# Linear attention and gated convolution FFN in one kernel: w_in loaded in three column blocks, identity between the first loads, an ordered factor product, another instruction order

## The chip, the cores and the metric

The kernel runs on one core of a Trainium2 chip. The core has TensorE (PE, with its weight loads shown as PEld), VectorE (DVE), ScalarE (ACT), GpSimd (POOL), SyncE (SP) and 16 DMA engines. The metric is the device time of one execution in microseconds; lower is better. "Time" is the whole execution; "span" is from the first to the last instruction of the profiled one.

## The reference

Eight batches, eight heads, 576 positions, head dimension 64; a model width of 512 and a hidden width of 1024. All inputs and the output are float32.

```python
kv  = einsum('bhsd,bhse->bhde', k, v)            # 64 x 64 per batch and head
out = einsum('bhsd,bhde->bhse', q, kv)
rms = sqrt(mean(out * out, axis=-1) + 1e-6)
x   = (out / rms * g_norm)                       # heads side by side: (b, 576, 512)

h    = maximum(x @ w_in, 0)                      # (b, 576, 1024)
conv = sum_k conv_w[k] * shift(h, k - 1)         # 3 taps along the positions, zero padded
y    = (h * sigmoid(conv)) @ w_out               # (b, 576, 512)
```

## The kernel before

**Layout.** A position s is split as s = p * 6 + r, so that q, k and v are loaded with 96 partitions (p) and six runs r of 64 values per head. POOL's queue loads them and casts float32 to bfloat16 on the way (`load`, L146 to L152). PE contracts k and v over the positions (`kv`, L263), two heads at a time into a 128 x 128 block diagonal `kvbd` (`kvc`), transposes q by an identity matrix (`qt`, L287; copied out by `qc`), and multiplies (`ot`, L310). The product has the model width on the partitions (four tiles t of 128) and the positions in the order (r, p) along the free dimension. `natural` (L315) is the view that reads them in the order p * 6 + r.

**Norm.** For batches 1 to 7 the squares (`sq`) are summed by PE (`ss`), ACT takes Ln and Exp (`ln`, `ex`), DVE splits the factors into bfloat16 parts (`sl`), PE spreads them over the partitions (`sp`), and DVE multiplies (`mu`, L415) into `xT`. Batch 0 has a shorter path, tile by tile: `sq`, a matmul with a block of ones (`on`), `nl` (Ln) and `nx` (Exp) over the full tile, and the product `mu0` (L358), which reads the product in PSUM and the factor `rs0` in SBUF, both in the order (r, p), and writes `xT` in the natural order, that is in steps of six bfloat16 values.

**FFN.** g_norm is folded into w_in: `ws` (L257) scales a staged float32 tile of w_in into the bfloat16 `w_in_sb`. `hm` (L427) is one 128-wide slice f of x @ w_in, `re` the relu. The convolution is done by PE for batch 0 (`di` builds diagonal matrices, `cv`, `sv`, `mv`: matmul, sigmoid, product) and by DVE for the others (`ta` three taps, `ad` two sums, `sg` sigmoid on ACT, `mg` product), in groups of one or two batches (CONV, L59). `om` multiplies a tile of 128 rows with w_out, `ea` evacuates it on ACT, `st` stores it from SP.

**Order.** Every engine runs its instructions in the order in which the program lists them. The program is a prologue (loads, constants) and then the list `ORDER` (L62 to L106), a text of some 640 tokens, each of which calls one of the functions above: `hm.3.5` is `hm(3, 5)`. The loop at L541 walks through the list, and the code at L546 ties each engine's instructions to that order. So the list sets the order on each of the engines and queues. PSUM is shared by two pools: `ps_a` with three buffers (qt, ot, on, sp, hm, cv) and `ps_b` with two (kv, ss, om, cw_ps).

**The prologue, before.** POOL issues q of batch 0 and then k and v in four chunks each (nine DMAs), makes the identity `ident` and a small float32 `ident32` (each a memset and an affine select, shown as masks.py lines), and then issues w_in as eight tiles of 128 x 512 float32 into the buffers `row` (L160). SP loads g_norm and the convolution weights (`cw_rows`). PE's first instruction transposes `cw_rows` by `ident32` into `cw_ps` (L207); DVE copies it to `cw` and derives `spread`, `ng`, `na`, `nb` from `ident` (L208 to L227). Activation tables are loaded by ACT when the function set changes (`act_table`, L229; "ln" and "sig").

Of the kernel before, what the change touches and what calls it, by code (L numbers as in the profile page):

```python
# [72 lines left out]
cv.0.3 sv.0.3 mv.0.6 sq.2.0 hm.1.1 re.1.1 ot.2.2 mv.0.7 ot.2.3 oc.2.3 mv.0.3 om.0.0 oc.2.2 ta.1.2 ta.1.3
ea.0.0 sq.2.2 Lv.3 Lq.3 ad.1.3 sg.1.3 kv.3.0.4 kvc.3.0.4.1 qt.3.1 Lk.4 ad.1.1 qc.3.1 qt.3.0 Lv.4 kvc.3.0.4.0
ot.3.3 qc.3.0 sg.1.1 mg.1.1 sq.2.3 sq.3.3 ot.3.2 oc.3.2 ot.3.1 oc.3.3 ta.1.4 sq.3.2 ta.1.5 om.0.2 sq.3.1
ad.1.2 ot.3.0 sq.3.0 hm.1.0 re.1.0 ss.2 ss.3 ln.1 ex.1 mg.1.3 ea.0.2 kv.4.0.4 Lq.4 Lk.5 Lv.5 sl.1 sp.2.0
mu.2.0 oc.3.1 oc.3.0 sp.3.0 sp.2.3 mu.3.0 om.0.3 mu.2.3 sp.2.2 mu.2.2 kvc.4.0.4.1 sp.2.1 mu.2.1 qt.4.1 sg.1.2
qc.4.1 ea.0.3 sp.3.1 om.0.1 kvc.4.0.4.0 ot.4.3 oc.4.3 sq.4.3 mu.3.1 sp.3.3 mu.3.3 hm.2.0 re.2.0 sp.3.2 qt.4.0
mu.3.2 qc.4.0 ot.4.2 hm.2.3 ta.1.0 ea.0.1 oc.4.2 sq.4.2 Lq.5 re.2.3 ot.4.0 oc.4.0 hm.2.1 ot.4.1 sq.4.0
kv.5.0.4 oc.4.1 re.2.1 ta.1.1 ad.1.0 hm.3.0 sq.4.1 kvc.5.0.4.0 Lk.6 re.3.0 kvc.5.0.4.1 sg.1.0 qt.5.0 st.0.0  # L80
qc.5.0 hm.2.2 re.2.2 mg.1.0 ot.5.0 oc.5.0 sq.5.0 qt.5.1 Lv.6 hm.3.3 Lq.6 Lk.7 Lv.7 re.3.3 qc.5.1 ot.5.2 oc.5.2
sq.5.2 hm.3.1 re.3.1 hm.3.7 Lq.7 re.3.7 ot.5.3 sq.5.3 mg.1.2 hm.3.4 re.3.4 ta.2.0 ta.2.1 ad.2.0 hm.3.2 oc.5.3
re.3.2 ot.5.1 sq.5.1 kv.6.0.4 ta.2.2 oc.5.1 ss.4 ss.5 ln.2 ex.2 ta.2.3 hm.3.5 re.3.5 hm.2.5 re.2.5 hm.2.4
re.2.4 sl.2 kvc.6.0.4.0 qt.6.1 qc.6.1 sp.4.0 qt.6.0 sp.5.1 mu.4.0 kvc.6.0.4.1 sg.2.0 om.0.7 qc.6.0 ot.6.1
mu.5.1 sp.4.3 mu.4.3 sp.5.2 ea.0.7 om.0.8 mu.5.2 oc.6.1 ot.6.0 hm.3.6 st.0.3 sq.6.1 ad.2.1 sq.6.0 sp.4.2
mu.4.2 ea.0.8 kv.7.0.4 sp.4.1 mu.4.1 oc.6.0 re.3.6 st.0.7 mg.2.0 ot.6.2 sg.2.1 kvc.7.0.4.0 sq.6.2 hm.2.6
re.2.6 qt.7.0 qc.7.0 st.0.2 kvc.7.0.4.1 oc.6.2 om.0.4 ea.0.4 ot.7.1 ot.6.3 ot.7.0 om.0.5 sq.6.3 ta.2.4 ta.2.5
# [22 lines left out]
def kernel(  # L110
# [43 lines left out]
    w_stage = {}  # L154

    def load_w_in(half):
        for t in range(NT):
# [2 lines left out]
            nc.gpsimd.dma_start(out=st, in_=moe_w_in[t * P:(t + 1) * P, half * 512:(half + 1) * 512])  # L160
# [424 lines left out]
```

## Time and profile before

| | |
|---|---|
| median of three runs | 217.47 us (217.29 to 218.61) |
| the profiled execution | 216.95 us, of which 215.2 us are the span |
| granted TensorE clock, mean | 0.992 |
| PE, DVE, ACT busy | 178.4, 158.3, 153.4 us |
| activation table loads | 10 (one in the prologue at L181, nine at L232) |
| HBM read, written | 32.52 MB, 9.44 MB |

A page of the profile gives busy times per engine, the span in 40 slices of 5.4 us with the busy share in tenths, the chain of work that ended last, and the groups of instructions by line. In a group's row stand line, engine, operation, output and input, shape and count, then the busy time in us and the mean of one in ns, then the idle time just before them and what ended it. "Idle before" is inferred from semaphores: a wait for several things is put down to the one that came last.

### The profile page before, as it was taken

How to read it: one execution, taken by the hardware profiler on the slowest of the kernel's cores; microseconds unless marked ns; L12 is line 12 of the kernel's file. 1: busy time of each engine (PE TensorE's matmuls, PEld its weight loads, DVE VectorE, ACT ScalarE, POOL GpSimd, SP SyncE). 2: the span in 40 equal slices, each digit the busy share in tenths (PEclk: the TensorE clock that was granted, in tenths of full speed). 3: DMA queues.
4: the chain of work that ended last, by engine and by line, in shares of the span. 5: the costliest groups of instructions: out<-in, count | busy, mean ns of one | idle time of the engine just before them, and what ended most of it. 6: DMA issues, size and time to landing. Idle time of an engine off the chain costs nothing.

```text
span 215.2 us, 4372 instructions
## 1 busy us (share of the span) xinstructions
PE 178.4 (83%) x1783; PEld 111.5 (52%) x1801; DVE 158.3 (74%) x328; ACT 153.4 (71%) x232; POOL 28.9 (13%) x47
## 2 busy tenths in 40 slices
PE   0246469957997839999989999999999999999993
...
DMA  5999999997089999399702000214130000324773
GB/s 61 198 322 263 204 206 204 138 201 116 3 121 202 213 182 186 82 138 196 111 5 97 3 0 0 101 41 155 49 149 0 0 3 0 148 97 154 282 269 126
DMA packets 25992, 27.03 MB, mean 126 GB/s; under 512 B 1372, under 2 KB 20852, under 8 KB 25972
## 3 DMA queue, kind: packets, MB, share of 16 engines
...
q1 hardware_dynamic: 5380, 9.45, 11.6%
q8 instruction: 14, 0.23, 0.5%
...
HBM read 32.52 MB, written 9.44 MB: 195 GB/s over the span
## 4 chain that ended last, share of the span: by engine, by line
DVE 39%; PE 37%; ACT 15%; issue 4%; DMA 3%; POOL 0%; POOLq 0%; ACTq 0%; DVEq 0%
PE h_ps L433 14%; PE om_ps L523 12%; DVE tap L458 12%; DVE tap L466 6%; DVE tap L465 5%; DVE h L478 4%; PE qt_ps L294 3%; DVE xT L360 3%; DMA q_sb<-in_q_dram 3%; PE cv_ps L499 3%; ACT sq L326 3%; ACT h L439 3%; DVE xT L416 3%; PE sp_ps L410 2%; ACT L232 2%
## 5 line engine op out<-in xcount | busy, mean ns | idle before, releaser
L433 PE MATMUL h_ps<-xT,w_in_sb 128*128 128x288 bf16 x512 | 70.1, 291 | 4.1 <-DVE xT L360 1.3
L523 PE MATMUL om_ps<-w_out_sb,h 128*128 128x512 bf16 x280 | 65.2, 385 | 0.8 <-issue 0.2
L433 PEld LDWEIGHTS <-w_in_sb 128*128 128x128 bf16 x512 | 50.0, 99 | 20.4 <-issue 5.4
L439 ACT ACTIVATE h<-h_ps 128x576 bf16<-128x576 f32 x64 | 40.2, 652 | 14.2 <-PE h_ps L433 13.7
L458 DVE TENSOR_SCALAR tap<-h,cw 128x576 bf16<-128x576 bf16 (+1 forms) x120 | 43.1, 425 | 4.2 <-ACT h L439 3.7
L523 PEld LDWEIGHTS <-h 128*128 128x128 bf16 x288 | 28.4, 99 | 33.4 <-issue 2.4
L472 ACT ACTIVATE tap<-tap 128x1152 bf16<-128x1152 bf16 (+1 forms) x20 | 30.9, 1547 | 3.9 <-DVE tap L466 3.7
L529 ACT ACTIVATE row<-om_ps 128x512 f32<-128x512 f32 x36 | 21.4, 594 | 17.1 <-PE om_ps L523 16.3
L416 DVE TENSOR_TENSOR xT<-o,sp_ps 128x576 bf16<-128x576 f32 x28 | 20.0, 748 | 6.0 <-PE sp_ps L410 6.0
L478 DVE TENSOR_TENSOR h<-h,tap 128x1152 bf16<-128x1152 bf16 (+1 forms) x20 | 19.8, 992 | 2.1 <-ACT tap L472 2.1
L466 DVE TENSOR_TENSOR tap<-tap 128x1150 bf16<-128x1150 bf16 (+1 forms) x20 | 20.1, 1004 | 0.7
L332 ACT ACTIVATE o<-o_ps 128x576 f32<-128x576 f32 x28 | 17.8, 659 | 3.3 <-PE o_ps L307 2.6
L465 DVE TENSOR_TENSOR tap<-tap 128x1150 bf16<-128x1150 bf16 (+1 forms) x20 | 19.8, 991 | 0.0
L326 ACT ACTIVATE sq<-o_ps 128x576 bf16<-128x576 f32 x28 | 17.7, 660 | 0.5 <-PE o_ps L307 0.5
L301 DVE COPY qT<-qt_ps 128x1152 bf16<-128x1152 bf16 x16 | 11.8, 751 | 6.9 <-PE qt_ps L294 6.9
L150 POOL DMA_DIRECT2D k_sb<-in_k_dram x11 | 8.0, 730 | 53.7 <-PE kv_ps L270 53.7
L284 ACT ACTIVATE kvbd<-kv_ps 64x256 bf16<-64x256 f32 (+1 forms) x18 | 6.1, 341 | 12.3 <-PE kv_ps L270 11.2
L306 PE MATMUL o_ps<-qT,kvbd 128*128 128x64 bf16 x32 | 6.3, 196 | 7.8 <-DVE kvbd L282 3.1
L410 PE MATMUL sp_ps<-wparts,spread 128*128 128x288 bf16 x56 | 10.0, 287 | 2.9 <-DVE wparts L401 2.7
L294 PE MATMUL qt_ps<-ident,q_sb 96*64 96x96 bf16 x384 | 11.5, 217 | 0.3
L232 ACT ACT_TABLE_LOAD x9 | 11.5, 1283 | 0.1
L294 PEld LDWEIGHTS <-q_sb 96*64 96x64 bf16 x384 | 9.8, 117 | 2.2 <-issue 2.1
...
## 6 DMA issues: line engine op xcount, KB each, us to landing
...
```

Of the source, the lines that this page charges most:

```text
L294: nc.tensor.transpose(ps[i * D:(i + 1) * D, tt, r * PS:(r + 1) * PS], q_sb[:, 2 * (2 * u + tt) + i, r * D:(r + 1) * D], ident[:PS, :PS])
L326: nc.scalar.activation(s.rearrange("p (n r) -> p n r", r=R), natural(src), AX.Square)
L416: nc.vector.tensor_mul(x_tile(b)[:, t, :].rearrange("p (e n) -> p e n", e=2), T["o32", b, t].rearrange("p (e n) -> p e n", e=2), T["sp", b ...
L433: nc.tensor.matmul(ps[:, e, :HS], w_in_sb[:, t, f * P:(f + 1) * P], x[:, t, e * HS:(e + 1) * HS], start=(t == 0), stop=(t == NT - 1))
L439: nc.scalar.activation(h_tile(b // 2)[:, f, b % 2, :].rearrange("p (e n) -> p e n", e=2), T["hm", b, f][:, :, :HS], AX.Relu)
L458: nc.vector.tensor_scalar_mul(tap[:, m, f % 2, :, :].rearrange("p b s -> p (b s)"), h_tile(p)[:, f, bs, :].rearrange("p b s -> p (b s)"), ...
L465: nc.vector.tensor_add(tap[:, 1, :, 1:], tap[:, 1, :, 1:], tap[:, 0, :, :S - 1])
L466: nc.vector.tensor_add(tap[:, 1, :, :S - 1], tap[:, 1, :, :S - 1], tap[:, 2, :, 1:])
L472: nc.scalar.activation(tap, tap, AX.Sigmoid)
L478: nc.vector.tensor_mul(h, h, T["tap", c, j][:, 1])
L523: nc.tensor.matmul(ps, h[:, f, m * P:(m + 1) * P], w_out_sb[:, f, :], start=(f == 0), stop=(f == NF - 1))
L529: nc.scalar.activation(T["os", p, m], T["om", p, m], AX.Copy)
```

## The change

- w_in is loaded as three column blocks (columns 0 to 255, 256 to 511, 512 to 1023), each one DMA for all 512 rows, into one staging tile of the pool tag `h`. The first is issued on SP's queue ahead of everything else there, the other two on POOL's queue behind k and v. `ws` scales a block at a time: three instructions instead of eight.
- DVE clears `ident` at the start; POOL's affine select follows the issue of q and stands ahead of k and v. `ident32` is a DVE copy of a corner of `ident`.
- `mu0` writes `xT` in order and reads its two inputs through `natural`.
- `ORDER` is replaced. The same functions are called with the same arguments, apart from `ws`. The list switches the activation table seven times instead of nine.

```diff
-di.5 qt.0.0 qc.0.0 qt.0.1 qc.0.1 kv.0.0.1 kvc.0.0.1.0 di.0 kv.0.1.1 kvc.0.1.1.0 kvc.0.0.1.1 ot.0.0 sq.0.0 di.6
-kvc.0.1.1.1 ot.0.1 sq.0.1 on.0 nl.0 nx.0 kv.0.2.1 kvc.0.2.1.1 kvc.0.2.1.0 on.1 kv.0.3.1 nl.1 nx.1 mu0.0 ot.0.2
-kvc.0.3.1.1 mu0.1 di.3 Lk.1 ws.3.0 Lv.1 kvc.0.3.1.0 ot.0.3 sq.0.2 ws.0.0 sq.0.3 on.2 nl.2 ws.1.0 nx.2 mu0.2
-ws.2.0 on.3 nl.3 nx.3 mu0.3 hm.0.0 re.0.0 di.7 Lq.1 ws.1.1 hm.0.2 ws.0.1 re.0.2 cv.0.0 sv.0.0 hm.0.1 re.0.1
-ws.2.1 ws.3.1 hm.0.5 re.0.5 di.2 cv.0.2 sv.0.2 hm.0.3 re.0.3 di.1 cv.0.1 mv.0.0 Lw sv.0.1 mv.0.2 cv.0.5 sv.0.5
-hm.0.7 kv.1.0.4 kvc.1.0.4.1 kvc.1.0.4.0 qt.1.1 qc.1.1 qt.1.0 qc.1.0 ot.1.3 re.0.7 oc.1.3 sq.1.3 Lk.2 Lv.2 Lq.2
-hm.0.4 re.0.4 ot.1.2 sq.1.2 ot.1.0 sq.1.0 mv.0.5 ot.1.1 sq.1.1 di.4 oc.1.2 mv.0.1 ss.1 ln.0 ex.0 sl.0 hm.0.6
-re.0.6 cv.0.7 oc.1.0 oc.1.1 sv.0.7 sp.1.0 mu.1.0 sp.1.2 mu.1.2 cv.0.6 sp.1.3 sp.1.1 mu.1.3 sv.0.6 Lk.3 cv.0.4
...
-re.5.1 mg.2.1 hm.5.0 re.5.0 st.0.4 hm.5.4 re.5.4 hm.4.4 re.4.4 ln.3 ex.3 ta.3.2 hm.4.6 mg.2.3 re.5.6 om.1.5
-ea.1.5 st.1.5 re.4.6 ta.3.3 om.1.6 ad.3.1 ea.1.6 sg.3.1 sl.3 ta.3.0 sp.7.0 sp.6.0 mu.7.0 sp.7.2 mu.7.2 om.1.7
...
+di.4 di.7 di.6 qt.0.0 qc.0.0 qt.0.1 kv.0.0.1 kvc.0.0.1.0 kvc.0.0.1.1 ot.0.0 di.5 kv.0.1.1 sq.0.0 qc.0.1 on.0
+di.2 kvc.0.1.1.0 nl.0 kvc.0.1.1.1 ot.0.1 sq.0.1 kv.0.2.1 nx.0 on.1 kvc.0.2.1.1 mu0.0 kvc.0.2.1.0 di.1 Lk.1
+Lv.1 nl.1 nx.1 kv.0.3.1 ot.0.2 kvc.0.3.1.1 sq.0.2 on.2 kvc.0.3.1.0 nl.2 mu0.1 ot.0.3 sq.0.3 on.3 ws.1 Lq.1
+ws.2 nx.2 mu0.2 nl.3 ws.0 nx.3 mu0.3 hm.0.0 hm.0.7 re.0.7 re.0.0 kv.1.0.4 kvc.1.0.4.0 Lw hm.0.5 Lk.2 Lv.2 Lq.2
+re.0.5 hm.0.2 re.0.2 qt.1.0 kvc.1.0.4.1 hm.0.4 re.0.4 qc.1.0 ot.1.0 qt.1.1 qc.1.1 ot.1.1 sq.1.0 oc.1.1 sq.1.1
+ot.1.2 sq.1.2 di.0 ot.1.3 sq.1.3 oc.1.3 oc.1.2 ss.1 ln.0 hm.0.1 Lk.3 ex.0 re.0.1 Lv.3 hm.0.6 di.3 Lq.3 oc.1.0
+hm.0.3 cv.0.0 re.0.6 sl.0 sp.1.0 mu.1.0 re.0.3 sv.0.0 cv.0.4 sp.1.1 kv.2.0.4 sv.0.4 Lk.4 sp.1.3 mu.1.1
+kvc.2.0.4.1 mv.0.0 mu.1.3 sp.1.2 mu.1.2 cv.0.6 cv.0.2 sv.0.6 hm.1.0 mv.0.6 qt.2.1 sv.0.2 mv.0.4 mv.0.2 qc.2.1
...
+oc.6.2 sq.6.2 ea.1.2 st.0.6 om.1.6 ot.7.0 sq.7.1 hm.4.4 om.1.8 sg.3.0 re.4.4 ea.1.6 sq.7.0 sq.7.3 ot.7.2
+st.1.2 ad.3.1 sq.7.2 ea.1.8 oc.7.3 om.1.3 ea.1.3 ss.6 ss.7 ln.3 hm.5.6 st.0.1 mg.3.0 ta.3.4 re.5.6 ta.3.5
+ad.3.2 om.1.4 hm.4.7 st.0.5 ex.3 om.1.0 oc.7.2 sl.3 oc.7.0 st.1.5 sp.6.0 mu.6.0 sp.6.3 re.4.7 mu.6.3 sg.3.1
...
-    from concourse.masks import make_identity
...
-    w_stage = {}
-
-    def load_w_in(half):
-        for t in range(NT):
-            st = work.tile([P, 512], FP32, name="row", bufs=BUFS["row"])
-            w_stage[t, half] = st
-            nc.gpsimd.dma_start(out=st, in_=moe_w_in[t * P:(t + 1) * P, half * 512:(half + 1) * 512])
-
+
+    W_COLS = ((0, 256), (256, 512), (512, 1024))
+    w_stage = work.tile([P, NT, D_ff], FP32, name="w_stage", tag="h", bufs=BUFS["h"])
+
+    def load_w_in(eng, i):
+        lo, hi = W_COLS[i]
+        eng.dma_start(
+            out=w_stage[:, :, lo:hi], in_=moe_w_in[:, lo:hi].rearrange("(t p) f -> p t f", p=P))
+
+    load_w_in(nc.sync, 0)
+    ident = consts.tile([P, P], BF16, name="ident")
+    nc.vector.memset(ident, 0.0)
     load("q", 0)
+    nc.gpsimd.affine_select(
+        out=ident, in_=ident, compare_op=AL.not_equal, fill=1.0,
+        base=0, pattern=[[-1, P]], channel_multiplier=1)
     for t in range(NT):
         load("k", 0, 2 * t, 2)
         load("v", 0, 2 * t, 2)
+    load_w_in(nc.gpsimd, 1)
+    load_w_in(nc.gpsimd, 2)
...
-    ident = consts.tile([P, P], BF16, name="ident")
-    make_identity(nc, ident)
     ident32 = consts.tile([3 * NF, 3 * NF], FP32, name="ident32")
-    make_identity(nc, ident32)
-    load_w_in(0)
-    load_w_in(1)
+    nc.vector.tensor_copy(ident32, ident[:3 * NF, :3 * NF])
...
     @op
-    def ws(t, half):
-        nc.vector.tensor_scalar_mul(
-            w_in_sb[:, t, half * 512:(half + 1) * 512], w_stage[t, half], g_sb[:, 0:1])
+    def ws(i):
+        lo, hi = W_COLS[i]
+        nc.vector.tensor_scalar_mul(w_in_sb[:, :, lo:hi], w_stage[:, :, lo:hi], g_sb[:, 0:1])
...
     @op
     def mu0(t):
-        x = x_tile(0)[:, t, :].rearrange("p (n r) -> p r n", r=R)
         nc.vector.tensor_mul(
-            x, T["ot", 0, t][:, :S].rearrange("p (r n) -> p r n", n=PS),
-            T["rs0", t].rearrange("p (r n) -> p r n", n=PS))
+            x_tile(0)[:, t, :].rearrange("p (n r) -> p n r", r=R),
+            natural(T["ot", 0, t][:, :S]), natural(T["rs0", t]))
```

More of the change, by code (lines that the diff above doesn't have):

```diff
@@ L73 @@
[L73 to L87, printed above, removed]
@@ new lines @@
+kvc.2.0.4.0 hm.1.1 re.1.0 re.1.1 ot.2.3 ta.1.0 cv.0.7 sq.2.3 sv.0.7 hm.1.4 Lv.4 oc.2.3 cv.0.5 qt.2.0 ta.1.1
+ad.1.0 re.1.4 sv.0.5 sg.1.0 hm.1.5 re.1.5 qc.2.0 ot.2.1 mg.1.0 cv.0.1 sq.2.1 sv.0.1 oc.2.1 ot.2.0 sq.2.0
+oc.2.0 kv.3.0.4 kvc.3.0.4.0 ta.1.4 Lq.4 qt.3.0 qc.3.0 hm.1.6 hm.1.7 kvc.3.0.4.1 ta.1.5 mv.0.7 re.1.6 re.1.7
+ot.3.0 oc.3.0 sq.3.0 mv.0.1 qt.3.1 cv.0.3 qc.3.1 ot.3.3 sv.0.3 oc.3.3 ta.1.6 Lk.5 Lv.5 ta.1.7 ot.3.2 sq.3.3
+sq.3.2 ot.3.1 oc.3.2 mv.0.3 ot.2.2 kv.4.0.4 sq.3.1 sq.2.2 oc.3.1 hm.1.2 ss.2 re.1.2 ss.3 ad.1.3 ln.1 ex.1
@@ new lines @@
+hm.3.5 re.3.5 ot.5.3 oc.5.3 sq.5.3 hm.3.2 hm.3.3 re.3.2 ot.5.0 hm.2.3 ta.2.4 re.3.3 sq.5.0 ta.2.5 re.2.3
+ot.5.2 sq.5.2 oc.5.0 oc.5.2 om.0.4 ot.4.0 ta.2.2 ot.5.1 hm.3.6 oc.4.0 ad.2.2 ta.2.3 sq.5.1 ea.0.4 sq.4.0
+om.0.5 ss.4 ss.5 oc.5.1 re.3.6 qt.6.0 ea.0.5 ln.2 qt.7.0 qt.6.1 ex.2 ad.2.1 qc.6.0 om.0.8 ea.0.8 sg.2.1 qc.6.1
+om.0.1 sl.2 sp.4.0 ea.0.1 sp.4.2 qc.7.0 sp.5.1 kv.6.0.4 mu.4.0 hm.3.0 mu.5.1 mu.4.2 mg.2.1 sp.5.0 hm.3.1
+mu.5.0 re.3.0 re.3.1 sp.4.3 kv.7.0.4 kvc.7.0.4.0 kvc.6.0.4.0 sp.5.3 kvc.7.0.4.1 hm.2.1 re.2.1 mu.4.3 ta.2.0
@@ new lines @@
+hm.2.6 sp.4.1 st.0.8 mu.5.3 kvc.6.0.4.1 sg.2.2 sp.5.2 ta.2.1 mu.4.1 om.0.7 hm.3.7 re.2.6 ad.2.0 mg.2.2 re.3.7
+sg.2.0 mu.5.2 om.0.6 hm.2.7 re.2.7 hm.4.0 ea.0.6 hm.5.1 ta.2.6 re.5.1 hm.4.3 re.4.3 ta.2.7 ea.0.7 hm.5.0
+re.5.0 re.4.0 hm.5.5 re.5.5 hm.5.2 re.5.2 st.0.3 ad.2.3 mg.2.0 st.0.7 qt.7.1 hm.4.1 hm.5.4 sg.2.3 re.4.1
+qc.7.1 re.5.4 hm.4.5 re.4.5 hm.4.2 ot.6.1 re.4.2 ta.3.0 oc.6.1 hm.5.3 sq.6.1 mg.2.3 ot.6.3 om.1.5 ot.6.0
+re.5.3 ot.7.1 oc.6.3 sq.6.3 ea.1.5 ot.6.2 sq.6.0 oc.7.1 om.1.2 ta.3.1 ta.3.2 oc.6.0 ta.3.3 ad.3.0 ot.7.3
```

34 lines of the change are left out of this document (16 added, 18 removed).

## The prediction

> **What bounds the kernel now.** I read the page first, then the busy times by stage, then the chain of waits of the first 30 us, then the groups by line.
>
> ```profile
> PE 178.4 (83%) x1783; PEld 111.5 (52%) x1801; DVE 158.3 (74%) x328; ACT 153.4 (71%) x232; POOL 28.9 (13%) x47
> PE   0246469957997839999989999999999999999993
> DMA  5999999997089999399702000214130000324773
> ```
>
> PE works 178.4 of 215.2 us, and nearly all its idle time lies in the first 15 of the 40 slices (80 us). The busy times by stage (us from the start; PE is the first busy column, then PEld, DVE, ACT, POOL, the granted clock, the DMA share and GB/s) put numbers on this:
>
> ```profile
> 0.00:9.50 9.50, 0.23 (x3) 0.19 (x3) 1.64 (x31) 1.28 (x1) 7.13 (x18) 1.00 0.85 120
> 9.50:29.30 19.80, 10.09 (x118) 5.40 (x119) 16.03 (x38) 8.74 (x16) 10.26 (x15) 1.00 1.22 252
> 29.30:52.00 22.70, 18.20 (x209) 12.73 (x210) 9.42 (x28) 17.91 (x28) 2.30 (x3) 1.00 1.19 183
> 52.00:80.00 28.00, 21.87 (x371) 15.62 (x373) 18.49 (x41) 23.01 (x40) 6.08 (x8) 1.00 0.87 136
> 80.00:145.00 65.00, 62.68 (x720) 41.29 (x728) 56.28 (x88) 58.29 (x91) 3.15 (x5) 0.97 0.45 79
> 145.00:201.00 56.00, 55.00 (x326) 31.90 (x327) 55.13 (x107) 38.91 (x51) 0.00 (x0) 1.00 0.22 83
> 201.00:215.20 14.20, 10.31 (x47) 4.40 (x45) 1.32 (x2) 5.22 (x8) 0.00 (x0) 1.00 0.59 224
> ```
>
> PE idles 9.3, 9.7, 4.5, 6.1, 2.3, 1.0 and 3.9 us in these seven stages. After 145 us PE and DVE are both full, so there a new order has nothing to win. What can be won lies before 80 us. The chain of waits of the first 30 us (start, length, what) says what holds the start:
>
> ```profile
> 1.29 6.11 DMA q_sb<-in_q_dram
> ...
> 8.60 0.29 POOL ident masks.py:199
> ...
> 9.60 0.18 DVE cw L208
> ...
> 12.07 0.57 DVE dg L487 x3
> ...
> 18.29 2.09 DVE xT L360
> ...
> 27.32 1.98 DVE xT L360
> ...
> 29.34 0.88 PE h_ps L433 x3
> ```
>
> q has landed at 7.40, but the identity, behind nine load issues on POOL, is ready only at 8.89. Then DVE prepares constants until 12.07 and scales conv diagonals (L487) before it serves q. From 18.29 the four products of batch 0 (L360) are the longest pieces, and the first matmul group of the FFN can finish only when the last of them ends, at 29.3.
>
> **The change part by part.** The groups by line (busy us, mean ns of one):
>
> ```profile
> L360 DVE TENSOR_TENSOR xT<-o_ps,o 128x576 bf16<-128x576 f32 x4 | 8.3, 2074 | 1.7 <-ACT o L350 1.7
> L416 DVE TENSOR_TENSOR xT<-o,sp_ps 128x576 bf16<-128x576 f32 x28 | 20.0, 748 | 6.0 <-PE sp_ps L410 6.0
> L332 ACT ACTIVATE o<-o_ps 128x576 f32<-128x576 f32 x28 | 17.8, 659 | 3.3 <-PE o_ps L307 2.6 <-PE qt_ps L294 0.6
> L324 ACT ACTIVATE sq<-o_ps 128x576 bf16<-128x576 f32 x4 | 2.6, 646 | 3.3 <-remote 2.9 <-PE o_ps L307 0.4
> L258 DVE TENSOR_SCALAR w_in_sb<-row,g_sb 128x512 bf16<-128x512 f32 x8 | 3.5, 483 | 0.0
> L346 ACT ACTIVATE o<-on_ps,eps_sb 128x576 f32<-128x576 f32 x4 | 3.0, 740 | 1.2 <-PE on_ps L307 1.2
> L350 ACT ACTIVATE o<-o 128x576 f32<-128x576 f32 x4 | 2.7, 683 | 0.1
> L232 ACT ACT_TABLE_LOAD x9 | 11.5, 1283 | 0.1
> L499 PE MATMUL cv_ps<-h,dg 128*128 128x288 bf16 (+1 forms) x48 | 7.5, 296 | 2.6 <-ACT h L439 1.7 <-DVE xT L416 0.7 <-ACT gate L507 0.2
> ```
>
> *The factor product (mu0).* It writes its 576 results in steps of 12 bytes and takes 2.07 us; L416 makes the same product of as many elements, written in order, in 0.75 us. The changed mu0 writes in order but reads both inputs in steps of 384 bytes. ACT reads PSUM in such steps (L332) in 0.66 us and in order (L324) in 0.65 us, so the step costs it nothing; DVE never reads so in this trace. Bounds: 0.75 us, and 2.07 us if the step costs on the read side what it costs on the write side, or somewhat more. I take 0.75, the same engine and operation. [...]
>
> *Identity and the SyncE block.* The rows for this part are the DMA rate in three single microseconds, and when w_in's rows and q were issued (length min/median/max in ns, first and last start) and landed:
>
> ```profile
> 2.00:3.00 1.00, 0.00 (x0) 0.00 (x0) 0.75 (x14) 0.03 (x1) 1.00 (x3) 1.00 0.13 6
> 11.00:12.00 1.00, 1.00 (x38) 1.00 (x36) 0.93 (x7) 0.01 (x1) 1.00 (x2) 1.00 1.30 197
> 13.00:14.00 1.00, 0.00 (x0) 0.00 (x0) 1.00 (x4) 0.00 (x0) 0.88 (x3) 1.00 1.01 410
> ...
> L160 POOL DMA_DIRECT2D row<-in_moe_w_in_dram x8: 537/538/1189, 9.2 to 13.8; - x8
> DMA to landing us min/median/max: 4.6/5.0/5.8
> ...
> L150 POOL DMA_DIRECT2D q_sb<-in_q_dram x3: 777/794/886, 1.3 to 20.5; - x3
> DMA to landing us min/median/max: 6.1/12.4/21.5
> ```
>
> The identity now follows q's issue (1.3 plus at most 0.9 us), so it is ready near 2.6 us by the 0.29 us of the old one; it pushes the k and v issues back 0.3 us, which hides in their queue. The block of w_in (512 KB) on SyncE's queue goes ahead of everything. The casting loads of q, k, v write 197 GB/s, the plain rows of w_in 410. 512 KB cost 1.3 us at 410 and 2.6 at 197; the engines are nearly idle before 3 us, so some of it is free: between 0 and 2.6, I take 1.0. q then lands at 8.4 and PE can start at once. g and cw_rows queue behind the block on SP and land, I estimate, near 6 us instead of before 9; PE's first instruction (cw_ps) waits for them, and behind it stand all of qt.0. If they land by 8 this is free. DVE's ident32 copy, new, waits for POOL's identity with the memsets of the constants behind it (1.64 us in the first stage); they end near 5 us and nobody needs them sooner. DVE's block behind cw (9.60 to 12.07, 2.5 us) then ends by 9, in the shadow of q. PE's first pieces, from two qt (48 matmuls) and two kv (24) to the first product with kvbd and the early matmuls of the FFN:
>
> ```profile
> 9.49 2.13 PE L294 MATMUL qt_ps<-ident,q_sb 96*64 96x96 bf16 x48
> 11.42 0.84 PE L270 MATMUL kv_ps<-v_sb,k_sb 96*64 96x64 bf16 x24
> ...
> 14.70 0.23 PE L306 MATMUL o_ps<-qT,kvbd 128*128 128x64 bf16 x1 [2.43 <-DVE kvbd L282]
> ...
> 25.76 1.12 PE L433 MATMUL h_ps<-xT,w_in_sb 128*128 128x288 bf16 x4 [0.83 <-ACT o L346]
> ...
> 27.38 0.66 PE L433 MATMUL h_ps<-xT,w_in_sb 128*128 128x288 bf16 x2 [0.50 <-DVE w_in_sb L258]
> ```
>
> That product started at 14.70. Now it starts two qt (2.1), one kv (0.4) and some 0.7 us for the copies and hand-offs behind q: 8.4 + 3.2 = 11.6 us. ACT then needs four times L324, L346 and L350 (2.07 us together): 8.3 us from 12.2, done near 21 with small gaps.
>
> *w_in in three pieces.* Its last bytes landed between 18.4 and 19.6 (13.8 plus 4.6 to 5.8); the bytes ahead of them in all queues are the same, so I take 19.0. Fewer issues on POOL (two instead of eight) gain nothing where DMA is full until 41 us. All of the scaling (3.5 us, taken as unchanged by the larger shapes) now stands before mu0.3: ws.1 and ws.2 (three quarters, 2.6 us) behind mu0.1, ws.0 (0.9) between mu0.2 and mu0.3. Before, half of it stood ahead. So DVE binds: 19.1 + 2.6 + 0.75 + 0.9 + 0.75 = 24.1 us for the last product, against 29.3. That is 5.2 us; but before, six of the eight matmuls of hm.0.0 had already run in the waits (25.76 and 27.38), worth 0.75 us of PE; now ws.0 comes too late for most of that. Net 4.5 us.
>
> *The order, 29 to 52 us.* ln.0 now stands ahead of sv.0.0, so the Ln table is still loaded, and two of the nine table loads fall away (2 x 1.28 us) in the stage where ACT works 17.9 of 22.7 us. These two pieces of the chain lie there:
>
> ```profile
> 45.84 1.28 ACT L232
> ...
> 50.49 0.77 DVE xT L416
> ```
>
> The load at 45.84 lies on the chain, and PE idled 4.5 us in this stage. Behind ss.1 now stand three hm (0.1, 0.6, 0.3), some 3 us that cover ln, ex and the split; three convolutions by matmul move behind sl.0 (3 x 6 x 0.296, at most 5.3 us) into the next stage. I take 2.0 of the 4.5 us.
>
> *52 to 80 us.* The moved convolutions fall where PE idles 6.1 us and ACT 5.0, so they cost nothing there unless that idle time goes to something else; I take a gain of 0.5. *After 80 us*: the same work in another order, all three engines nearly full: 0, from +1 to -3. At the end five om still stand behind the last mg, as before.
>
> *Loads.* They stay in the same order on POOL. The third q landed at 20.5 + 21.5 = 42.0; qt.2.1 will now want it near 43. So batch 2's load becomes the next thing that is late if the middle goes better than I think.
>
> The sum: 4.5 + 2.0 + 0.5 = 7.0 us off the profiled execution's 216.95 gives 209.95. The median of the runs shown is 0.5 above that execution, so I forecast 210.5.
>
> **The rivals.** A, the forecast (0.48): 210.5, by the bounds above 208.5 to 213.
>
> B, the later idle time closes too (0.18): the norm chain of batches 2 and 3 is covered as batch 1's is, and PE wins 4 of its 6.1 us between 52 and 80: 206.5. For it: there also PE waits while ACT works 23.0 of 28. Against it: ACT gets the deferred gates in that stage.
>
> C, mu0 stays at 2.07 us (0.14). DVE then runs mu0.1 18.4 to 20.5, ws until 23.1, mu0.2 to 25.2, ws.0 to 26.1, mu0.3 to 28.2: 4.1 us later than in A, 214.6. [...] With a read that costs still more, about 216.
>
> D, the start is won and lost again (0.12): after 80 us DVE idled 8.7 + 0.9 us and PE 2.3 + 1.0; any waits that the new order adds there count in full, and seven of them give 217.5. This is also the case that the change does not do what it says.
>
> E, slower (0.08): DVE starves ahead of sl.3. In the new order ta.3.0, ta.3.1, ta.3.4, ta.3.5, two ad and mg.3.0 stand ahead of sl.3 on DVE, and no longer behind it. If they wait on sigmoid or relu of a PE that is itself behind, sl.3 and so all of batches 6 and 7 (mu, hm, conv) come late. It decides once DVE's 8.7 us of idle time between 80 and 145 grows by more than 7; doubled and a little more, the time is 210.5 + 9.5 = 220.
>
> **How the numbers follow.** The likeliest case gives 210.5. The range 205 to 216 takes in B's lower side and C, and leaves out part of D, E and the fringe of B, about 2 in 10. One per cent, about what a measurement of this kernel can tell from no change, is 2.2 us. Faster (below 215.3): A, B, somewhat more than half of C and a little of D, 0.76. Within 1%: the rest of C and most of D, 0.14. Slower: E and a little of D, 0.10.
>
> **What would show it.** cw_ps well before q lands, q at 8 to 9, first product with kvbd near 11.6. L360 (now a new line) at 0.75 us mean. Last mu0 ending near 24. Eight table loads of L232 and L181 together instead of ten. The first L416 near 43 instead of 50.49. PE idle between 52 and 80 no larger than 6, and the last five om starting near 195. I am wrong if cw_rows lands after q, if L360's successor stays near 2 us, or if DVE's idle time after 80 us grows.

## The result

The changed kernel takes 204.42 us (median of four runs, 203.46 to 205.56) against 217.57 before: a ratio of 0.939, 95% interval 0.934 to 0.944. The prediction said 210.5, between 205 and 216. The direction was right, the gain was 13.1 us instead of 7.0, and the time lies 0.6 us below the range. The profiled execution took 203.46 us, of which 201.4 us are the span.

The page of the changed kernel, in the lines that are shown of the kernel before, with the granted clock:

```profile
PE 175.6 (87%) x1783; PEld 111.7 (55%) x1801; DVE 155.5 (77%) x325; ACT 149.9 (74%) x230; POOL 25.3 (13%) x38
PE   0057389799998999999999999999999999999792
PEclk9999999999999999999999999999999999999999
DMA  5999999999999999970200020080005001423654
```

PE is now nearly full from the sixth slice on (the DMA engines are full until slice 17: the loads no longer pause). PE's busy time itself fell by 2.8 us, with the same 1783 instructions; for about half of that the reason comes below (a stretch at half clock in the kernel before). The busy times by stage, with the last two cut where DVE now ends:

```profile
0.00:9.50 9.50, 0.04 (x1) 0.07 (x1) 1.84 (x33) 1.28 (x1) 5.73 (x13) 1.00 0.78 132
9.50:29.30 19.80, 12.01 (x126) 7.33 (x129) 14.73 (x40) 8.60 (x16) 7.87 (x10) 1.00 1.24 234
29.30:52.00 22.70, 21.00 (x297) 15.27 (x298) 11.43 (x28) 17.89 (x32) 3.84 (x5) 1.00 1.30 204
52.00:80.00 28.00, 26.57 (x418) 18.11 (x419) 24.42 (x49) 26.86 (x46) 7.05 (x9) 1.00 1.26 196
80.00:145.00 65.00, 64.37 (x655) 42.20 (x661) 60.36 (x90) 59.92 (x89) 0.77 (x1) 1.00 0.28 68
145.00:190.00 45.00, 43.69 (x259) 25.41 (x262) 42.74 (x88) 32.34 (x45) 0.00 (x0) 1.00 0.23 88
190.00:201.40 11.40, 7.90 (x37) 3.37 (x35) 0.00 (x0) 2.99 (x5) 0.00 (x0) 1.00 0.60 230
```

PE idles 9.5, 7.8, 1.7, 1.4, 0.6, 1.3 and 3.5 us. Before 29.3 us that is only 1.7 us less than in the kernel before; between 29.3 and 80 us it is 3.1 instead of 10.6. So most of the gain is not where the prediction's sum put it.

The clock column needs care at the start. It reads 1.00 there, but the trace has no clock record before 30.75 us (32.50 in the kernel before), and sixteen matmuls of one shape take about twice as long ahead of that time as behind it:

```profile
25.73 4.02 PE L434 MATMUL h_ps<-xT,w_in_sb 128*128 128x288 bf16 x16 [2.21 <-DVE w_in_sb L261]
...
30.99 2.13 PE L434 MATMUL h_ps<-xT,w_in_sb 128*128 128x288 bf16 x16
```

So in both kernels PE's matmuls run at 0.5 to 0.6 of their later speed in the first 30 us: in the kernel before, ten of this shape take 2.56 us at 29.34 and sixteen 2.12 at 32.83, 48 of the transposes (qt) take 2.13 us at 9.49 and 1.22 at 67.43, and a 128x512 matmul of ot 0.61 us at 15.61 and 0.38 at 70.50. What is measured there on PE costs about that share of it later.

The chain of the first 30 us says why the start gave so little:

```profile
2.42 6.91 DMA cw_rows<-in_moe_conv_w_dram
...
9.46 0.28 PE cw_ps L209
...
12.14 1.47 DVE dg L488 x9
...
18.77 1.16 DVE xT L361
...
25.73 4.02 PE h_ps L434 x16
```

cw_rows lands at 9.33, not near 6. PE's first instruction and, behind it, DVE's constants and nine diagonal scalings (three in that place before) come as late as before, and the first product with kvbd starts at 14.58 (14.70 before). The two groups that the change was to make cheaper:

```profile
L361 DVE TENSOR_TENSOR xT<-o_ps,o 128x576 bf16<-128x576 f32 x4 | 4.6, 1141 | 0.7 <-ACT o L352 0.6
...
L234 ACT ACT_TABLE_LOAD x7 | 9.0, 1283 | 0.1
```

The product takes 1.14 us, neither 0.75 nor 2.07; the table loads are 8 in all, as counted.

**Where the 13.8 us of the span went.** Four sections can be cut at events that both kernels have: the end of the last mu0, and the first instruction of the factor split `sl` for batch 1 (sl.0) and for batches 2 and 3 (sl.1). DVE's timeline has the split (start, length, line; idle before). Before:

```profile
48.15 0.31 DVE L398 CAST hi<-rs 128x288 bf16<-128x288 f32 x1 [4.93 <-ACT rs L390]
...
77.73 0.31 DVE L398 CAST hi<-rs 128x288 bf16<-128x288 f32 x1 [2.23 <-ACT rs L390]
```

After:

```profile
40.42 0.31 DVE L399 CAST hi<-rs 128x288 bf16<-128x288 f32 x1 [2.93 <-ACT rs L391]
...
68.37 0.31 DVE L399 CAST hi<-rs 128x288 bf16<-128x288 f32 x1 [0.46 <-ACT rs L391]
```

| section (us) | before | after | gain | forecast |
|---|---|---|---|---|
| start to the end of the last mu0 | 29.29 | 26.71 | 2.6 | 5.2 |
| to sl.0 | 18.86 | 13.71 | 5.2 | 1.25 (2.0 less 0.75) |
| to sl.1 | 29.58 | 27.95 | 1.6 | 0.5 |
| to the end of the span | 137.5 | 133.0 | 4.4 | 0 |

### The profile page after: what moved, and what is told of

Read it like the earlier page. It is cut to its first block, busy times and chain, and to the rows that moved or that the text cites. A ratio compares the mean times of both kernels' runs of the same rounds, so it can differ in the third digit from the quotient of the medians.

```text
span 201.4 us, 4356 instructions
## 1 busy us (share of the span) xinstructions
PE 175.6 (87%) x1783; PEld 111.7 (55%) x1801; DVE 155.5 (77%) x325; ACT 149.9 (74%) x230; POOL 25.3 (13%) x38
## 3 DMA queue, kind: packets, MB, share of 16 engines
q1 hardware_dynamic: 5908, 9.98, 13.1%
## 4 chain that ended last, share of the span: by engine, by line
PE 60%; DVE 26%; ACT 6%; DMA 3%; issue 2%; SPq 1%; DVEq 0%; ACTq 0%
PE h_ps L434 25%; PE om_ps L524 18%; DVE tap L459 8%; DVE h L479 4%; PE qt_ps L296 4%; DMA cw_rows<-in_moe_conv_w_dram 3%; DVE tap L467 3%; PE kv_ps L272 3%; PE sp_ps L411 3%; DVE tap L466 3%; PE cv_ps L500 3%; PE o_ps L309 2%; DVE xT L417 2%; ACT tap L473 2%; DVE dg L488 2%
## 5 line engine op out<-in xcount | busy, mean ns | idle before, releaser
L524 PE MATMUL om_ps<-w_out_sb,h 128*128 128x512 bf16 x278 | 64.1, 379 | 1.5 <-DVE h L479 1.0
L440 ACT ACTIVATE h<-h_ps 128x576 bf16<-128x576 f32 x64 | 41.0, 656 | 13.5 <-PE h_ps L434 13.2
L459 DVE TENSOR_SCALAR tap<-h,cw 128x576 bf16<-128x576 bf16 (+1 forms) x120 | 43.8, 429 | 1.7 <-ACT h L440 1.3
L530 ACT ACTIVATE row<-om_ps 128x512 f32<-128x512 f32 x36 | 22.1, 616 | 15.1 <-PE om_ps L524 14.5
L417 DVE TENSOR_TENSOR xT<-o,sp_ps 128x576 bf16<-128x576 f32 x28 | 20.1, 749 | 4.0 <-PE sp_ps L411 3.7
L328 ACT ACTIVATE sq<-o_ps 128x576 bf16<-128x576 f32 x28 | 18.2, 687 | 0.5 <-PE o_ps L309 0.5
L286 ACT ACTIVATE kvbd<-kv_ps 64x256 bf16<-64x256 f32 (+1 forms) x18 | 6.0, 339 | 11.8 <-PE kv_ps L272 11.6
L296 PE MATMUL qt_ps<-ident,q_sb 96*64 96x96 bf16 x384 | 11.2, 217 | 1.2 <-DMA q_sb<-in_q_dram 0.9
L272 PEld LDWEIGHTS <-k_sb 96*64 96x64 bf16 x384 | 7.9, 122 | 3.3 <-issue 3.3
## 6 DMA issues: line engine op xcount, KB each, us to landing
k_sb<-in_k_dram POOLq DMA_DIRECT2D x7, 576.0 KB, 10.6
```

The costliest lines, as they stand in the source:

```text
L296: nc.tensor.transpose(ps[i * D:(i + 1) * D, tt, r * PS:(r + 1) * PS], q_sb[:, 2 * (2 * u + tt) + i, r * D:(r + 1) * D], ident[:PS, :PS])
L328: nc.scalar.activation(s.rearrange("p (n r) -> p n r", r=R), natural(src), AX.Square)
L417: nc.vector.tensor_mul(x_tile(b)[:, t, :].rearrange("p (e n) -> p e n", e=2), T["o32", b, t].rearrange("p (e n) -> p e n", e=2), T["sp", b ...
L440: nc.scalar.activation(h_tile(b // 2)[:, f, b % 2, :].rearrange("p (e n) -> p e n", e=2), T["hm", b, f][:, :, :HS], AX.Relu)
L459: nc.vector.tensor_scalar_mul(tap[:, m, f % 2, :, :].rearrange("p b s -> p (b s)"), h_tile(p)[:, f, bs, :].rearrange("p b s -> p (b s)"), ...
L524: nc.tensor.matmul(ps, h[:, f, m * P:(m + 1) * P], w_out_sb[:, f, :], start=(f == 0), stop=(f == NF - 1))
```

## The experiments

The kernel before, measured again beside the kernels below, has medians of 217.0 to 217.2 us, and 217.57 beside the changed kernel; so a difference of half a microsecond between two medians means little. The same cuts, from the timeline of one profiled execution of each (first product is the first with kvbd; lengths in us):

| kernel | median | first product | mu0 ends | to sl.0 | to sl.1 | to the end |
|---|---|---|---|---|---|---|
| before | 217.47 | 14.70 | 29.29 | 18.86 | 29.58 | 137.5 |
| order alone | 207.69 | 14.69 | 30.86 | 13.49 | 27.95 | 133.2 |
| order undone | 214.42 | 15.25 | 26.54 | 18.73 | 29.59 | 137.3 |
| changed kernel | 204.42 | 14.58 | 26.71 | 13.71 | 27.95 | 133.0 |
| gates first | 207.66 | 14.55 | 27.16 | 18.36 | 26.58 | 133.1 |
| two more tables | 208.26 | 15.47 | 27.62 | 16.49 | 29.43 | 133.1 |
| cover undone | 208.37 | 14.95 | 27.51 | 13.71 | 30.91 | 133.1 |
| product undone | 206.78 | 15.96 | 31.43 | 13.44 | 27.95 | 133.1 |
| small loads on ACT's queue | 202.76 | 14.07 | 26.20 | 12.84 | 27.96 | 133.0 |
| block 0 behind cw_rows | 201.57 | 11.74 | 25.42 | 12.86 | 27.95 | 133.1 |
| all of w_in on POOL | 201.24 | 10.81 | 25.20 | 12.70 | 27.95 | 133.2 |
| same, block 2 scaled last | 200.20 | 11.12 | 23.36 | 13.70 | 27.95 | 133.1 |

The columns hardly mix: the first is set by the loads, the products and the scaling, the other three mostly by the order. One thing crosses over: in the last four rows PE comes to its full speed (the first clock record) 1.8 to 2.1 us behind the last mu0, in the changed kernel 4.0 us behind it, and the first sixteen matmuls of hm take 3.45 to 3.60 us against 4.02. In three of them the section to sl.0 is 0.85 to 1.0 us shorter, about what 2 us less at half speed are worth; in the fourth PE waits for a load instead.

### The order alone, and all but the order

The kernel before with only the new list; its eight scalings stand where the list scales blocks:

```diff
-... mu0.1 ot.0.3 sq.0.3 on.3 ws.1 Lq.1 ws.2 nx.2 mu0.2 nl.3 ws.0 nx.3 mu0.3 ...
+... mu0.1 ot.0.3 sq.0.3 on.3 ws.0.0 ws.1.0 ws.2.0 ws.3.0 Lq.1 ws.0.1 ws.1.1 ws.2.1 ws.3.1 nx.2 mu0.2 nl.3 nx.3 mu0.3 ...
```

> The kernel before with only the new order (w_in still in eight tiles on POOL's queue, scaled at the places where the new order scales its blocks; identity behind the loads; the product as before). Theory 1, the order is most of the gain (it packs ACT and the loads between 29 and 80 us): 207 to 210 us, PE idle between 30 and 80 us near 4 us, table loads 8. Theory 2, the start (loads, identity, product) is most of it, as the prediction's sum had it: 213 to 215 us, PE idle between 30 and 80 us above 7 us.

The changed kernel with the old list, with ws.0, ws.1 and ws.2 in place of ws.3.0, ws.2.0 and ws.1.1, and the other five scalings left out of the list:

> The changed kernel with the old order (blocks scaled where the old order scaled tiles; all else changed). Theory 1: 213 to 216 us, PE idle between 30 and 80 us near 10 us as in the kernel before. Theory 2: 209 to 211 us. If the parts only add, this and the run with the order alone split the 13.1 us between them; if order and start help each other, the two gains together fall short of 13.1.

The order alone takes 207.69 us (ratio 0.957, 0.950 to 0.964), 9.5 us less; all but the order 214.42 us (0.987, 0.981 to 0.993), 2.8 us less. Theory 1 holds. The two add up to 12.3 of the 13.1 us, so the parts hardly help or hinder each other. The stages from 29.3 to 80 us of the order alone:

```profile
29.30:52.00 22.70, 19.77 (x258) 13.86 (x258) 9.69 (x20) 15.09 (x27) 3.84 (x5) 1.00 1.22 187
52.00:80.00 28.00, 26.51 (x399) 17.82 (x403) 23.90 (x51) 25.91 (x45) 5.67 (x7) 1.00 1.21 182
```

and of the order undone:

```profile
29.30:52.00 22.70, 17.99 (x219) 12.91 (x219) 8.05 (x17) 18.42 (x29) 2.30 (x3) 1.00 1.21 190
52.00:80.00 28.00, 21.89 (x358) 14.87 (x361) 19.14 (x41) 23.84 (x39) 6.14 (x8) 0.95 0.96 147
```

PE idles 4.4 us in the first and 10.8 in the second. With the old loads the new order is even 1.6 us later at the last mu0 (30.86 against 29.29), since it puts all of the scaling ahead of it; it wins 5.4, 1.6 and 4.3 us behind.

### What in the order: the gates, the table loads, the cover

Three of batch 0's gates moved back ahead of batch 1's norm in the changed kernel:

```diff
-... hm.0.4 re.0.4 qc.1.0 ot.1.0 qt.1.1 qc.1.1 ot.1.1 ...
+... hm.0.4 re.0.4 cv.0.4 sv.0.4 cv.0.2 sv.0.2 cv.0.5 sv.0.5 qc.1.0 ot.1.0 qt.1.1 qc.1.1 mv.0.4 mv.0.2 mv.0.5 ot.1.1 ...
```

> The changed kernel with three of batch 0's convolutions and gates (slices 4, 2 and 5: cv, sv, mv) moved back ahead of batch 1's norm, as the old order had four; that also brings the table loads back from 8 to 10 in all. Theory A: the order wins because batch 1's norm chain no longer stands behind gates and their table loads on ACT: sl.0 comes 3 to 4 us later, and the time rises by 3 to 5 us to 207.5 to 209.5. Rival: the deferred gates only changed places with other work, ACT and PE do the same amount before the FFN of batch 1: 204 to 205.5 us.

207.66 us, 3.2 more. DVE's timeline:

```profile
45.52 0.31 DVE L398 CAST hi<-rs 128x288 bf16<-128x288 f32 x1 [3.25 <-ACT rs L390]
...
72.10 0.31 DVE L398 CAST hi<-rs 128x288 bf16<-128x288 f32 x1 [0.46 <-ACT rs L390]
```

sl.0 comes 4.65 us later behind the last mu0, and only 1.4 us of that comes back before sl.1, because the moved work then is done. Theory A holds: that section is the gates and tables ahead of the norm chain on ACT, 18.36 us with them, 18.86 in the kernel before, 13.71 without. (The next run has a price for the two table loads alone: 2.78 of these 4.65 us.)

Two more table loads ahead of ln.0, nothing else:

```diff
     def ln(g):
         ...
+        if g == 0:
+            nc.scalar.preload_act_table_set("sigmoid_and_others")
+            nc.scalar.preload_act_table_set("natural_log_exp_and_others")
         act_table("ln")
```

> The changed kernel with two more activation table loads ahead of ln.0 and nothing else changed (10 in all, 2.6 us of ACT's time). Theory: the two loads saved are on the chain and each is worth its 1.28 us: 206.5 to 207 us. Rival: the three hm behind ss.1 cover them in part: at most +1 us, 204.5 to 205.5.

208.26 us, 3.8 more: not less than the theory but more than it. The chain has both loads, 2.56 us in a row:

```profile
40.52 1.28 ACT L387
...
41.81 1.28 ACT L388
```

The section to sl.0 grows by 2.78, as it should, but the next one by 1.48 too. PE's busy time and granted clock (the first value after the length is PE, the third from the end is the clock) say why:

```profile
42.00:44.00 2.00, 0.13 (x2) 0.00 (x0) 0.00 (x0) 1.96 (x4) 0.00 (x0) 1.00 1.31 203
44.00:46.00 2.00, 1.33 (x9) 0.97 (x9) 1.66 (x4) 1.70 (x4) 0.00 (x0) 0.88 1.31 203
46.00:48.00 2.00, 2.00 (x10) 1.25 (x9) 0.01 (x1) 1.97 (x3) 0.00 (x0) 0.50 1.31 204
```

PE stands still for 2.54 us, and soon behind that works at half clock (0.50 in the third row). The kernel before has the same behind its gap ahead of sl.1, which is two waits with a kv between them:

```profile
77.27 0.95 PE L270 MATMUL kv_ps<-v_sb,k_sb 96*64 96x64 bf16 x48 [1.95 <-ACT rs L386]
79.55 0.92 PE L410 MATMUL sp_ps<-wparts,spread 128*128 128x288 bf16 x6 [1.32 <-DVE wparts L401]
```

```profile
76.00:80.00 4.00, 1.40 (x52) 1.30 (x52) 1.67 (x5) 3.92 (x8) 1.47 (x2) 1.00 1.24 192
80.00:84.00 4.00, 3.78 (x14) 1.68 (x14) 2.07 (x3) 2.24 (x3) 0.07 (x1) 0.57 1.19 157
```

That is a clock of 0.57 over 4 us (one record of 3.41 us at 0.50, from 80.29), or 1.7 us of work lost behind the idle time. What stood ahead of the slow stretch was 2.54 us of standing still with two more tables, and in the kernel before 1.95 and 1.32 us with 0.95 us of work between them.

Not every execution has the slow stretch. Of the eleven executions of the kernel before that were measured beside the kernels "small loads on ACT's queue" and "block 2 scaled last", three have a mean granted clock of 1.000 (215.7 to 215.8 us), six of 0.992, which is one such stretch as in the profiled one (216.9 to 217.8 us), and two of 0.984 (218.3 and 219.0 us). So one stretch costs the kernel before about 1.3 us. All four executions of the run with two more tables and of the order undone have it; of the other kernels with the new order only the one without the cover (next) has executions below 0.997.

By the profile the 4.4 us of the last section are 1.4 us of PE's busy time (128.9 against 127.5 us from sl.1 to the end) and 3.0 us less idle time, of which the wait for wparts (1.32 us) still lies ahead of 80 us. The split is rough, since the work behind sl.1 is not quite the same: two qt and part of a kv in the kernel before, two om in the changed one. The order undone has the slow stretch too and, with 137.3 us, the same last section as the kernel before.

The cover of the second norm chain taken away, by moving two transposes and an hm ahead of it:

```diff
-... hm.1.2 ss.2 re.1.2 ss.3 ad.1.3 ln.1 ex.1 ... qt.4.1 qt.4.0 ad.1.2 mv.0.5 qc.4.1 hm.1.3 qc.4.0 ... re.1.3 ...
+... qt.4.1 qc.4.1 qt.4.0 qc.4.0 hm.1.3 re.1.3 hm.1.2 ss.2 re.1.2 ss.3 ad.1.3 ln.1 ex.1 ... ad.1.2 mv.0.5 ...
```

> The changed kernel with the two qt of batch 4 and hm.1.3 moved from behind ss.3, where they cover the norm chain of batches 2 and 3, to ahead of ss.2 (2.1 us of PE). Theory B: the cover is worth what it lasts, PE idles 2 us more between 52 and 80 us and the time rises by 1.5 to 2.5 us to 206 to 207. Rival: ACT, not PE, is the bound of this stage (26.9 of 28 us), ss then comes when ACT is ready anyway: 204 to 205 us.

208.37 us, 3.9 more by the medians. The profiled executions differ by 3.7: 2.96 in the section to sl.1 and 0.8 in a later start (mu0 ends 0.8 us later, before the edit can act). PE's timeline names the two waits that appear:

```profile
66.36 0.70 PE L295 MATMUL qt_ps<-ident,q_sb 96*64 96x96 bf16 x24 [0.92 <-ACT o L333]
...
71.67 1.89 PE L523 MATMUL om_ps<-w_out_sb,h 128*128 128x512 bf16 x7 [1.95 <-ACT rs L386]
```

Together 2.9 us. Theory B holds in kind: PE's cover counts in full although ACT is as full in that stage (26.86 us against PE's 26.57 of 28 in the changed kernel). Its range was too low; three of the four executions have a mean clock of 0.988 to 0.990 (207.8 to 209.4 us), the profiled one 1.000 (207.14 us).

### The product

The changed kernel with L358 to L362 of the kernel before in place of the new mu0:

> The changed kernel with the factor product written as before (steps of 12 bytes). Theory: four products at 2.07 instead of 1.14 us, three of them in a row with the scaling of w_in on DVE, so the FFN's first group starts 2 to 2.8 us later and the time is 206.5 to 207.5. Rival: ACT or the landing of w_in (22 us) sets the start and hides the products: 204 to 205 us.

206.78 us, 2.4 more, as the theory had it. The product's group and its last instruction:

```profile
L362 DVE TENSOR_TENSOR xT<-o_ps,o 128x576 bf16<-128x576 f32 x4 | 8.3, 2078 | 0.9 <-ACT o L352 0.8
```

```profile
29.36 2.07 DVE L362 TENSOR_TENSOR xT<-o_ps,o 128x576 bf16<-128x576 f32 x1
```

The last mu0 ends 4.7 us later than in the changed kernel, of which 1.3 were there before the first one (20.04 against 18.77), so the stretch of the four products is 3.4 us longer. The profiled execution is the longest of four (205.83 to 207.87 us). The other sections do not move.

### The block of w_in ahead of everything

Block 0 on SP's queue behind g and cw_rows:

```diff
-    load_w_in(nc.sync, 0)
     ident = consts.tile([P, P], BF16, name="ident")
...
     nc.sync.dma_start(out=cw_rows, in_=moe_conv_w.rearrange("k (f p) -> (k f) p", p=P))
+    load_w_in(nc.sync, 0)
```

> The changed kernel with SyncE's block of w_in issued behind g and cw_rows on the same queue. Theory: the block ahead of them made cw_rows land at 9.3 us and with it delayed DVE's constants and the first diagonals; with it behind, cw_rows lands near 4.5 us, cw_ps runs before q lands, and the first product with kvbd starts 1 to 2 us before 14.6. If the start sets the end, the time falls by 1 to 2 us to 202.5 to 203.5. Rival: q itself lands at 10.6 us because the block shares the DMA engines, so nothing moves: 204 to 205 us, q still at 10.5.

201.57 us (0.929, 0.923 to 0.935), 2.9 less than the changed kernel. cw_ps runs at 5.99 and PE starts on q at 7.72 instead of 10.61: so the block had delayed q too, as the rival had it, but only from its place ahead of everything. The time lies below both ranges.

All three blocks on POOL's queue:

```diff
-    load_w_in(nc.sync, 0)
...
+    load_w_in(nc.gpsimd, 0)
     load_w_in(nc.gpsimd, 1)
     load_w_in(nc.gpsimd, 2)
```

> The changed kernel with all three blocks of w_in on POOL's queue behind k and v. Theory: without the block q lands at 7.4 us as in the kernel before, the first product with kvbd starts near 11.6 to 12.5 us, w_in lands near 20 us, the FFN's first group starts 2 us earlier, the time is 202 to 203 us. Rival: the same bytes have to land before the FFN starts, so w_in's last block is as late as now (22 us) and the time stays at 204 to 205 us although the first product is earlier.

201.24 us (0.928, 0.922 to 0.934). The first product is at 10.81, 3.8 us earlier, but the last mu0 only 1.5. The time lies below both ranges, but both theories hold a part: the start moves, and then the landing of w_in binds. DVE's timeline:

```profile
21.17 1.29 DVE L261 TENSOR_SCALAR w_in_sb<-w_stage,g_sb 128x2048 bf16<-128x2048 f32 x1 [1.98 <-DMA w_stage<-in_moe_w_in_dram]
22.37 1.12 DVE L361 TENSOR_TENSOR xT<-o_ps,o 128x576 bf16<-128x576 f32 x1
```

What delays q? g and cw_rows moved to ScalarE's queue, with the block still first on SP's:

```diff
-        nc.sync.dma_start(out=g_sb[i * D:(i + 1) * D, :], in_=g_norm.unsqueeze(1))
+        nc.scalar.dma_start(out=g_sb[i * D:(i + 1) * D, :], in_=g_norm.unsqueeze(1))
...
-    nc.sync.dma_start(out=cw_rows, in_=moe_conv_w.rearrange("k (f p) -> (k f) p", p=P))
+    nc.scalar.dma_start(out=cw_rows, in_=moe_conv_w.rearrange("k (f p) -> (k f) p", p=P))
```

> The changed kernel with g and cw_rows issued on ScalarE's queue instead of behind the block of w_in on SyncE's; the block stays ahead of q. It tells apart why q and cw_rows landed late (10.6 and 9.3 us). Theory 1, the block itself takes the DMA engines from q: q still lands at 10 to 10.6 us, the time is 203.5 to 204.5. Theory 2, the tiny transfers queued behind the block on the same rings hold up the engines between 4 and 8 us: q lands by 8.5 us, cw_ps runs by 6, and the time is near that of the kernel with the block behind cw_rows, 201.5 to 202.5.

q still serves PE only at 11.05, so it is not the small transfers: theory 1 in that point. cw_rows is late as well, though it no longer stands behind the block on a queue: cw_ps runs at 8.92, against 5.99 with the block behind cw_rows. But theory 1's picture, a block that takes the engines, is not right either. The DMA share and rate (last two columns) of single microseconds in this kernel:

```profile
3.00:4.00 1.00, 0.00 (x0) 0.00 (x0) 0.64 (x18) 1.00 (x1) 1.00 (x3) 1.00 0.68 193
4.00:5.00 1.00, 0.00 (x0) 0.00 (x0) 0.77 (x11) 0.07 (x1) 1.00 (x2) 1.00 0.21 36
5.00:6.00 1.00, 0.00 (x0) 0.00 (x0) 0.00 (x0) 0.00 (x0) 1.00 (x3) 1.00 0.93 89
```

and with all of w_in on POOL:

```profile
3.00:4.00 1.00, 0.00 (x0) 0.00 (x0) 0.65 (x18) 0.00 (x0) 1.00 (x3) 1.00 0.87 76
4.00:5.00 1.00, 0.00 (x0) 0.00 (x0) 0.77 (x11) 0.00 (x0) 1.00 (x2) 1.00 1.20 178
5.00:6.00 1.00, 0.27 (x1) 0.18 (x1) 0.00 (x0) 0.00 (x0) 1.00 (x3) 1.00 1.28 198
```

With the block first, the engines are nearly idle between 4 and 5 us (a share of 0.21), when most of the block has moved (281 and 193 GB/s in the two microseconds before) and q's load has been issued for two microseconds; q flows only from 5 us on. In the changed kernel itself, with g and cw_rows behind the block on SP's queue, the engines have a share of 1.05 in that microsecond but move only 104 GB/s. What holds q's first bytes back is open. The time, 202.76 us, is 1.7 below the changed kernel by the medians, but the executions overlap (202.02 to 204.32 against 203.46 to 205.56 us); the profiled ones differ by 0.5 us in the start and 0.9 in the section to sl.0, where PE comes to its full speed earlier (first clock record at 28.22 us against 30.75; the first sixteen matmuls of hm take 3.58 us against 4.02).

### A faster version

On top of all of w_in on POOL, block 2 is scaled behind mu0.3, and hm.0.2, which needs block 1 alone, changes places with hm.0.7:

```diff
-... ws.1 Lq.1 ws.2 nx.2 mu0.2 nl.3 ws.0 nx.3 mu0.3 hm.0.0 hm.0.7 re.0.7 re.0.0 ... re.0.5 hm.0.2 re.0.2 ...
+... ws.1 Lq.1 nx.2 mu0.2 nl.3 ws.0 nx.3 mu0.3 ws.2 hm.0.0 hm.0.2 re.0.0 re.0.2 ... re.0.5 hm.0.7 re.0.7 ...
```

> The kernel with all of w_in on POOL's queue, and ws.2 moved behind mu0.3 on DVE, with hm.0.2 in hm.0.7's place on PE as the second group (hm.0.7 needs block 2). There DVE waited 2 us for block 2 with mu0.2, ws.0 and mu0.3 behind it. Theory: mu0.3 ends 1 to 2 us earlier, near 23.5, and the time falls by 1 to 1.5 us from 201.2 to 199.7 to 200.3. Rival: hm.0.2, hm.0.7 and kv.1 then wait for the scaling of block 2 or for the loads of batch 1, and the time stays at 201 to 201.5.

200.20 us (0.926, 0.921 to 0.931 against the kernel before), in the theory's range. The last mu0 ends at 23.36:

```profile
22.24 1.12 DVE L360 TENSOR_TENSOR xT<-o_ps,o 128x576 bf16<-128x576 f32 x1
23.28 1.28 DVE L260 TENSOR_SCALAR w_in_sb<-w_stage,g_sb 128x2048 bf16<-128x2048 f32 x1
```

That is 1.8 us earlier, of which 1.0 is given back before sl.0 (PE then waits 0.87 us for v of batch 1). The interval overlaps that of the step before it.

## Why the prediction was wrong

*What bounds the kernel: right in the main.* Idle PE time before 80 us was the larger part of what could be won. It fell from 29.6 us to 20.4.

*The start, 4.5 us net: wrong.* The first section gave 2.6 us, not 5.2. The step that failed is the price of the SyncE block: q was taken to land at 8.4 and served PE at 10.61, and cw_rows at 6 and landed at 9.33. The text had named the condition (cw_rows by 8 is free); it was not met. The chain shown with the result runs through cw_rows; q alone, at 10.61 plus the 3.2 us that the sum had behind it, would have put the first product at 13.8 instead of 14.58, so either load alone was late enough to undo most of this term. The sum treated the block as bytes in a shared pipe; the runs show a delay of 3 us for q (PE starts on it at 10.61, and at 7.43 with all of w_in on POOL) that the 1.3 to 2.6 us put on the block's bytes don't explain. Identity and ident32 were priced rightly: cw_ps waits for cw_rows, not for them.

*The landing of w_in, 19.0: wrong too, but hidden.* POOL issued its ninth load only when the first, q, had landed (it waited 3.95 us for it), and w_in stood behind that:

```profile
10.85 0.78 POOL L148 DMA_DIRECT2D v_sb<-in_v_dram  x1 [3.95 <-DMA q_sb<-in_q_dram]
11.63 1.55 POOL L158 DMA_DIRECT2D w_stage<-in_moe_w_in_dram  x2
```

The last block landed at 22.0 us, and in the runs with column blocks that show it at 20.6 (the order undone) at the earliest. In the changed kernel DVE is not ready for it any earlier. With all of w_in on POOL, where q lands at 7.4, DVE does wait for it (21.1), and the last product ends at 25.20 and not at 24.1. One more term had the wrong size: six early matmuls of hm.0.0 were put at 0.75 us of PE, but the two rows quoted for them are 1.12 and 0.66 us long.

*The product, 0.75 us: too low.* 1.14 us lies between the bounds, nearer the lower one, and costs about 0.4 us four times over what was taken. The read in steps of 384 bytes costs 0.39 us here (1.14 against 0.75 us in order), the write in steps of 12 bytes more (2.07). Which of the two inputs costs it, the one in PSUM or the one in SBUF, no run tells apart. Rival C did not come. Undoing the product costs 2.4 us by the medians and 3.4 from the first product to the last in the profiled execution, between two and four times the 0.94 us between 2.08 and 1.14.

*The order from 29 to 52 us, 2.0 us: mechanism right, size wrong.* Table loads and gates leave ACT ahead of the norm chain, exactly as described. The first L417 starts at 43.22, as forecast ("near 43"), but that is luck: the start gave 2.6 us less than forecast and this section 3.9 more. The section is 5.2 us shorter and not 1.25: the term was capped at 2.0 of the stage's 4.5 us of idle time, though the same change also moves the gates' convolutions out of the section.

*52 to 80 us, 0.5 us, and rival B.* The moved convolutions were indeed absorbed, and the stage's idle time fell from 6.1 to 1.4 us. B (0.18) has the mechanism that the runs show: the second norm chain is covered, and taking the cover away costs 2.96 us.

*After 80 us, 0: wrong.* It gave 4.4 us from sl.1 on, of which 1.3 are the last wait ahead of 80 us, so about 3 lie behind, the edge of what the text allowed (+1 to -3). Two things were missed. The gap ahead of sl.1 is followed by 4 us at a clock of 0.57, which the stage row quoted in the prediction has as 0.97 over 65 us; closing a gap pays for the slow matmuls behind it. And the idle PE time behind 80 us could still fall, from 7.2 to 5.5 us.

So by the four sections the forecast under-weighed the order by 9.4 us (1.75 against 11.2) and over-weighed the start by 2.6. B's 206.5 was still 2.1 us too slow: it had the better middle, but also the start that did not come, and not the clock.
